# Opening's transposed weights in other tiles, weights' splits behind the scores; no decoding around the middle, lower parts shared out

## The chip, the cores and the metric

The kernel runs on one core of a Trainium2 chip. The metric is the time in device microseconds of that core. Of the kernel before there are three runs: 711.22, 711.5 and 713.99 us, median 711.5 us.

## The reference

Three blocks follow one another; all inputs are float32, apart from the weights of the last block, which the kernel receives in double precision.

```python
# attention: q, k, v of (2, 8, 576, 64)
scores = scale * np.matmul(q, k.transpose(0, 1, 3, 2))
mask_plain = (rel >= 0) & (rel < window)                                       # heads 0-3, window 32
mask_dil = (rel >= 0) & (rel < window * dilation) & (rel % dilation == 0)      # heads 4-7, dilation 4
attn = np.exp(scores - np.max(scores, axis=-1, keepdims=True))                 # masked
attn = attn / (np.sum(attn, axis=-1, keepdims=True) + 1e-09)
x = np.matmul(attn, v)                                                         # -> (1152, 512)
# four experts, all of them computed for every token
for e in range(4):
    h = np.maximum(x @ w1[e], 0.0)            # w1[e] 512 x 1024
    out += p[:, e:e + 1] * (h @ w2[e])        # w2[e] 1024 x 512
# last block
h = x @ w_in                                  # 512 x 2048
g = h - np.tanh(h)
result = g @ w_out                            # 2048 x 512
```

## The kernel before, in words

**Arithmetic.** Each matrix product is three passes of reduced fp32 (type fp32r): an operand is split into a high part (a copy, on ScalarE) and a lower part (a subtraction, on VectorE or GpSimd), and the passes are high x high, high x low, low x high. From the third weight slice on, the first product of a pair is cut in the Strassen-Winograd manner into 7 products of half blocks, whose results are added up on VectorE and GpSimd (`sums_of`; the addition L708 of p5 to u on GpSimd).

**Passes.** The tokens are two sets, g=0 (512 tokens) and g=1 (640). There are 14 passes n, each over one slice of weights: n=0..7 serve set 0 with the experts' 8 slices, n=2..9 set 1 (so n=2..7 serve both, n=8 and 9 only set 1); n=10..13 are the four slices of the last block, called tanh passes here, for both sets. A pass has its h's (14 half products per set, matmuls at L730 for the first two passes and at L782 after) and its y's (one per 128 tokens, 12 matmuls of 128x512 at L825, added to `acc` at L846). `merge` puts the y's of one set between the h's of the other, at the places of `FIRST` and `THEN`.

**Order.** A planner adds up guessed durations of these steps (`duration`, `start`), and everything else is given a due time by `when` and emitted as its due time passes; `later` does the same relative to the step just emitted. Each engine then executes what was emitted in that order. So a table of due times decides what stands before what on VectorE, ScalarE, GpSimd and the SP queue.

**Opening.** `first_attention` runs set 0's four pairs of heads through scores (L480), `largest` (L496), `exps`, `norm` (L519), `transposes` (L527, result copied at L530), `values` (L563) and copying into xf (L567). The result of the transposes lies in the second half t[:, 1] of the same `att` tile that holds the weights; there are four such tiles. Set 1's pairs follow within the first weight passes, one every `BEAT` = 11 planned us.

**Decoding.** w_in and w_out come as doubles. 32 tiles are decoded to fp32: `d_load`, then `d_decode` with one tensor_scalar (L660) and three two-input instructions (L664, L672, L677) on VectorE, one square (L671) on ScalarE, and a store; the list `where` holds the 32 due times.

**Between the experts and the last block.** `x2_step` transposes `acc` into x2f (L871, L875), and `x2_prep` splits it. In the tanh passes `hidden` takes tanh (L762), b - tanh in PSUM (L128), the high part (L769) and the lower part (L128), where `sub` at L128 is the common subtraction.

Of the kernel before, what the change touches and what calls it, by code (L numbers as in the profile page):

```python
# [10 lines left out]
F32R = mybir.dt.float32r  # L11
I32 = mybir.dt.int32
BF16 = mybir.dt.bfloat16
ACTF = mybir.ActivationFunctionType
# [58 lines left out]
def tile_local_attention_moe_tanhshrink(  # L73
# [392 lines left out]
    class Pair:  # L466


        def __init__(self, kind, c, banks):
            self.h, self.c, self.banks = kind, c, banks  # L470
            self.kk = c if kind.plain else 2 + c
            self.n = NST[kind.g]
            self.lag = kind.g
            self.t = {}

# [47 lines left out]
        def transposes(self, a):  # L523
            pb = bank(self.banks["t"])
            t = self.t[a]
            for j in range(4):
                nc.tensor.transpose(  # L527
                    pb[:BK, j * 128:(j + 1) * 128], t[:, 0, j * BK:(j + 1) * BK], ident
                )
            nc.scalar.activation(out=t[:BK, 1], in_=pb[:BK], func=ACTF.Copy)  # L530

# [9 lines left out]
        def values(self, i):  # L541
# [4 lines left out]
            for tile_, j, t, o in h.values()[i]:  # L546
                for a in range(2):
                    f0 = j * 4 * D + (2 * self.c + a) * D
                    n = 32 if tile_ == "short" else BQ
                    if t < 512:  # L550
                        w = self.t[a][:BK, 1, t:t + n]
                    else:
                        w = self.t[0][:BK, 0, a * 128 + t - 512:a * 128 + t - 512 + n]
                    if isinstance(o, tuple):
                        at, step, m = o
                        to = xb[D * a:D * a + D, at:at + step + m]
                        to = xb[D * a:D * a + D, at - 128:at - 128 + 2 * step].rearrange(
                            "c (r p) -> c r p", p=step
                        )[:, :, 128:128 + m]
                        w = w.rearrange("k (r p) -> k r p", p=m)  # L560
                    else:
                        to = xb[D * a:D * a + D, o]
                    nc.tensor.matmul(  # L563
                        out=to, lhsT=h.v[tile_][:BK, f0:f0 + D], rhs=w, start=True, stop=True,
                    )
# [38 lines left out]
    def w_sum(n, name, engine):  # L604
# [9 lines left out]
        else:  # L614
            sub(engine, block(n, "a21"), block(n, "a11"), block(n, "a21"))

    def w1_split(n, name, engine, lag=1.0):
        t = w1t[n, name] = w1p.tile([128, 2, 2, 256], F32R, tag="w1", name="w1")
        src = sums[n] if name in ("s1", "s2", "s4") else block(n, {"s3": "a21"}.get(name, name))
        split(t[:, 0], t[:, 1], src, engine, lag, ("w1", n, name))  # L620
# [121 lines left out]
    def place(g, what):  # L742
# [6 lines left out]
        ring[what] += 1  # L749
        t, i = (store[2], i % 3) if what == "th" else (store[i // 3 % 2], i % 3)  # L750
        return t[:, i * 320:i * 320 + QH[g]]

    def hidden(n, g, f, half, b, done):
# [7 lines left out]
        th = place(g, "th")  # L761
        nc.scalar.activation(out=th, in_=b, func=ACTF.Tanh)  # L762

        def lower():
# [151 lines left out]
    for n in range(N2 + 1, LAST + 1):  # L916
        steps += merge(hs(n, 0), ys(n - 1, 1), FIRST) + merge(hs(n, 1), ys(n, 0), THEN)
    steps += ys(LAST, 1)
# [24 lines left out]
    for n in range(1, len(seq)):  # L943
        after = []
        if n < EARLY:
            t0 = start["h", n - 1, 0, 0]

            for i, name in enumerate(("a11", "a12", "a21", "a22")):
                when(t0 + 5.0 + 1.8 * i, lambda n=n, name=name: w1_split(n, name, nc.gpsimd),
                     ("w1", n, name))  # L950
# [23 lines left out]
    where = []  # L974
    for n, m in [(n, 4) for n in range(EARLY + 1, NS1)] + [(N2, 4), (N2 + 1, 4)]:
        a, b = period(n)
        where += [a + (b - a) * (i + 0.3) / m for i in range(m)]
        if n == NS1 - 1:
            a = start["y", n, 1, 0]
            where += [a + 13.0 * i + 2.0 for i in range(4)]  # L980
    order_d = [o + 4 * s + i for s in range(4) for o in (0, 16) for i in range(4)]
# [10 lines left out]
    for g, due, step in (  # L992
        (0, start["y", NS1 - 1, 1, 0] + 0.1, 5.0),
        (1, start["y", N2 - 1, 1, SETS[1][1] // 128 - 1] + 2.73 + 1.5, 2.8),
# [14 lines left out]
    def first_attention():  # L1009
# [4 lines left out]
        def call(k, stage):  # L1014
            pair, a = head(k)
            getattr(pair, stage)(a)

        pairs[0].scores()
        w1_split(0, "a11", nc.vector)
        pairs[1].scores()  # L1020
        for k in range(8):
            call(k, "largest")
            if k:
                call(k - 1, "norm")
            if k == 1:
                w1_split(0, "a12", nc.gpsimd)
            if k > 1:
# [23 lines left out]
    for n in range(4):  # L1051
        pair = Pair(kinds[1, n < 2], n % 2, {"s": "s", "t": "a", "x": "a"})
        due = BEAT * n
        when(due, pair.scores)
# [11 lines left out]
    for c in range(2):  # L1066
        when(BEAT * 3 + 17.0 + 4.0 * c, lambda c=c: prep(1, c, True, nc.vector, nc.gpsimd), ("x", 1, False))
    for c in range(2):
# [5 lines left out]
    with tc.manual_schedule():  # L1074
# [5 lines left out]
        pa.load_k(0)  # L1080
        w_load(0, 0)
        pa.load_q(slice(1, 2))
        pa.load_k(1)
        w_load(0, 1)
        da.load_q()
        for u in range(2):
            da.load_k_cut(u)
        for i in range(2):
            pa.load_v(i)
        for i in range(2):  # L1090
# [102 lines left out]
```

## Time and profile before

| what | value |
|---|---|
| median of three runs | 711.5 us |
| profiled execution | 711.79 us |
| its span, first to last instruction | 710.0 us |
| TensorE busy | 637.2 us (90%) |
| VectorE busy | 449.0 us (63%) |
| ScalarE busy | 293.7 us (41%) |
| GpSimd busy | 355.9 us (50%) |
| mean granted TensorE clock | 0.945 |

The time outside the span is 1.8 us. The slices of the page show TensorE at 90% or more over most of the span, and lower at the start, near 60% of the span, and at about 70% of it.

### The profile page before, as it was taken

The numbers are of one execution on the slowest core, as the hardware profiler recorded it, in microseconds if no ns is written. First come the engines' busy times: TensorE is split into PE (matmuls) and PEld (weight loads), VectorE is DVE, ScalarE is ACT, GpSimd is POOL, SyncE is SP. The second block draws the span as 40 slices with busy tenths as digits, with TensorE's granted clock in tenths as the row PEclk, the third lists the DMA queues.
The fourth block names the chain that finished last, engine by engine and source line by source line (L and its number), as shares of the span: only waits on it lengthen the run. The fifth ranks groups of instructions, "written<-read, shape, count | busy, mean of one in ns | idle before, by whom it ended". The sixth has DMA issues, their size and how long they took to land.

```text
span 710.0 us, 10901 instructions
## 1 busy us (share of the span) xinstructions
PE 637.2 (90%) x4063; PEld 559.0 (79%) x4063; DVE 449.0 (63%) x892; ACT 293.7 (41%) x656; POOL 355.9 (50%) x319
## 2 busy tenths in 40 slices
PE   5486999899999999999999995969695998999997
PEld 3375787797988989889899893948594887998995
DVE  4449463744795877857858857554757378465672
ACT  2344554534542434424424453332555454353530
POOL 4347596653662733816627478472365354372400
PEclk8658999999999999999999997979898999999999
DMA  8941111201225133242252514231313313200012
GB/s 316 321 133 60 60 61 61 90 0 55 96 69 185 65 128 108 87 161 91 76 177 71 181 46 137 71 104 44 105 45 104 104 45 117 91 31 1 1 45 90
DMA packets 36694, 68.07 MB, mean 96 GB/s; under 512 B 4128, under 2 KB 10400, under 8 KB 36640
## 3 DMA queue, kind: packets, MB, share of 16 engines
q1 hardware_dynamic: 36640, 67.37, 27.9%
q8 instruction: 32, 0.52, 0.3%
q14 instruction: 22, 0.18, 0.1%
HBM read 56.61 MB, written 10.75 MB: 95 GB/s over the span
## 4 chain that ended last, share of the span: by engine, by line
PE 60%; DVE 10%; POOL 6%; issue 3%; ACT 2%; DVEq 0%; POOLq 0%; ACTq 0%
PE bank_f L825 21%; PE bank_f L782 16%; PE bank_s L825 11%; PE bank_s L782 5%; PE bank_a L825 3%; PE bank_a L782 3%; POOL w L128 3%; DVE single L664 1%; POOL sum L128 1%; DVE h L128 1%; DVE single L672 1%; DVE bank_f L708 1%; POOL sums L708 1%; DVE h L714 1%; DVE bank_f L128 1%
## 5 line engine op out<-in xcount | busy, mean ns | idle before, releaser
L825 PE MATMUL bank_f<-w,h 128*128 128x512 f32 x864 | 215.9, 399 | 11.8 <-ACT h L711 7.0
L128 POOL TENSOR_TENSOR w<-raw,w 128x512 fp32r<-128x512 f32 x109 | 145.7, 1340 | 120.6 <-ACT w L165 106.4
L825 PEld LDWEIGHTS bank_f<-w,h 128*128 128x128 f32 x864 | 160.3, 191 | 48.6 <-ACT h L711 8.3
L782 PE MATMUL bank_f<-x,w 128*128 128x320 f32 (+1 forms) x1224 | 182.7, 302 | 2.7 <-DVE h L128 2.2
L782 PEld LDWEIGHTS bank_f<-x,w 128*128 128x128 f32 x1224 | 175.1, 193 | 7.9 <-DVE h L128 2.6
L708 POOL TENSOR_TENSOR sums<-u,p 128x320 f32<-128x320 f32 (+1 forms) x44 | 38.6, 880 | 133.0 <-DVE u L708 133.0
L825 PE MATMUL bank_s<-w,h 128*128 128x512 f32 x324 | 82.9, 406 | 17.2 <-ACT h L769 7.1
L165 ACT ACTIVATE w<-raw 128x512 fp32r<-128x512 f32 x112 | 69.1, 628 | 42.9 <-PE bank_f L825 22.4
L825 PEld LDWEIGHTS bank_s<-w,h 128*128 128x128 f32 x324 | 61.4, 195 | 32.1 <-ACT h L769 7.6
L846 DVE SCALAR_TENSOR_TENSOR acc<-bank_f,pn,acc 128x512 f32<-128x512 f32 x42 | 31.4, 747 | 48.8 <-PE bank_f L825 48.8
L782 PE MATMUL bank_s<-x,w 128*128 128x320 f32 (+1 forms) x396 | 60.2, 297 | 0.6 <-ACT x2f L875 0.6
L782 PEld LDWEIGHTS bank_s<-x,w 128*128 128x128 f32 x396 | 56.4, 189 | 2.5 <-ACT x2f L875 0.9
L128 POOL TENSOR_TENSOR w<-sum,w 128x512 fp32r<-128x512 f32 x36 | 50.3, 1396 | 6.2 <-ACT w L165 6.2
L711 ACT ACTIVATE h<-bank_f 128x320 fp32r<-128x320 f32 (+2 forms) x83 | 35.1, 428 | 43.4 <-DVE bank_f L708 39.1
L714 DVE SCALAR_TENSOR_TENSOR h<-bank_f,h 128x320 fp32r<-128x320 f32 (+2 forms) x83 | 38.9, 473 | 11.4 <-ACT h L711 10.5
L165 ACT ACTIVATE w<-sum 128x512 fp32r<-128x512 f32 x36 | 22.8, 632 | 47.9 <-POOL sum L128 27.8
L794 ACT ACTIVATE p<-bank_f 128x320 f32<-128x320 f32 (+1 forms) x60 | 23.7, 416 | 45.3 <-PE bank_f L782 45.1
L782 PE MATMUL bank_a<-x,w 128*128 128x320 f32 (+1 forms) x228 | 37.2, 299 | 0.1
L782 PEld LDWEIGHTS bank_a<-x,w 128*128 128x128 f32 x228 | 33.7, 191 | 1.6 <-DVE h L714 0.4
L677 DVE SCALAR_TENSOR_TENSOR single<-double,single 128x512 f32<-128x512 f32 x32 | 26.0, 812 | 12.3 <-ACT double L671 11.4
L664 DVE SCALAR_TENSOR_TENSOR single<-double,single 128x512 int32<-128x512 int32 x32 | 32.4, 1013 | 1.1
L730 PE MATMUL bank_f<-x,w 128*128 128x256 f32 x192 | 29.0, 308 | 4.3 <-ACT x L165 4.3
(125 smaller groups left out, 820.7 us busy)
## 6 DMA issues: line engine op xcount, KB each, us to landing
raw<-in_moe_w_dram SPq DMA_DIRECT2D x40, 512.0 KB, 5.3
double<-in_moe_w_in_dram SPq DMA_DIRECT2D x16, 512.0 KB, 3.8
double<-in_moe_w_out_dram SPq DMA_DIRECT2D x16, 512.0 KB, 3.5
in<-single SPq DMA_DIRECT2D x16, 256.0 KB, 2.6
out<-single SPq DMA_DIRECT2D x16, 256.0 KB, 2.1
raw<-in SPq DMA_DIRECT2D x8, 512.0 KB, 6.0
raw<-out SPq DMA_DIRECT2D x8, 512.0 KB, 4.8
h<-in_v_dram SPq DMA_DIRECT2D x7, 512.0 KB, 8.2
```

Source lines behind the costliest of these rows:

```text
L128: engine.tensor_tensor(out=out, in0=a, in1=b, op=ALU.subtract)
L165: nc.scalar.activation(out=hi, in_=src, func=ACTF.Copy)
L664: nc.vector.scalar_tensor_tensor(out=t, in0=high, scalar=-0x40000000, in1=t, op0=ALU.bitwise_and, op1=ALU.bitwise_or)
L677: nc.vector.scalar_tensor_tensor(out=w, in0=mag, scalar=HIGH_MIN * HIGH_MIN, in1=w, op0=ALU.is_ge, op1=ALU.mult)
L708: e.tensor_tensor(out=o, in0=x, in1=y, op=ALU.add)
L711: nc.scalar.activation(out=hi, in_=src, func=ACTF.Relu)
L714: nc.vector.scalar_tensor_tensor(out=lo, in0=src, scalar=0.0, in1=hi.bitcast(F32), op0=ALU.max, op1=ALU.subtract)
L730: nc.tensor.matmul(out=b, lhsT=w[:, wi, kk % 2, f % 2 * 128:(f % 2 + 1) * 128], rhs=x[:, kk % 2, xi, :], start=(kk == 0 and m == 0), stop= ...
L782: nc.tensor.matmul(out=b, lhsT=w[:, wi, kk, t * 128:(t + 1) * 128], rhs=x[:, kk, xi, :], start=(kk == 0 and i == 0), stop=(kk == 1 and i = ...
L794: nc.scalar.activation(out=pt[P], in_=b, func=ACTF.Copy)
L825: nc.tensor.matmul(out=y, lhsT=a, rhs=b_, start=(f == 0 and m == 0), stop=(f == NF - 1 and m == 2),)
L846: nc.vector.scalar_tensor_tensor(out=t, in0=y, scalar=p, in1=t, op0=ALU.mult, op1=ALU.add)
```

## The change

1. The transposed weights of set 0's pairs 0 to 2 go to new tiles "pt" out of the w1 pool, so that an `att` tile is free once it has been transposed and not only after `values`. The tiles of n=0's w1 are placed ahead, and the splits of its first two blocks come behind `largest` of heads 2 and 3; the lower part of both is GpSimd's. The loads stand in another order.
2. The w1 splits of n=1 are due 6 us later, set 1's attention 3 us later.
3. Decoding: 5 tiles a pass instead of 4 in n=3..6, 4 in n=7, none from there to n=11, 5 in n=11 and 3 in n=12 (before: 4 in each of n=3..7, 4 behind n=7, 4 in n=10 and 4 in n=11).
4. Set 0's `x2_step`s are 2.7 planned us apart instead of 5.0.
5. In the tanh passes, for one of the two halves of each block of h, b - tanh is written over the tanh in SBUF, and the lower part is GpSimd's.
6. The first y's of n=11 stand 3 products later.

```diff
@@ transposes
-            nc.scalar.activation(out=t[:BK, 1], in_=pb[:BK], func=ACTF.Copy)
+            if self.lag == 0 and self.kk < 3 and a == 0:
+                far = plain32(w1p.tile([128, 2, 2, 256], F32R, tag="w1", name="pt"))
+                self.pt = {0: far[:, :512], 1: far[:, 512:]}
+            to = self.pt.setdefault(a, t[:, 1])
+            nc.scalar.activation(out=to[:BK], in_=pb[:BK], func=ACTF.Copy)
@@ values
-                        w = self.t[a][:BK, 1, t:t + n]
+                        w = self.pt[a][:BK, t:t + n]
@@ place: where tanh (th) and u5 lie
-        t, i = (store[2], i % 3) if what == "th" else (store[i // 3 % 2], i % 3)
+        t, i = (store[1 + i // 3 % 2], i % 3) if what == "th" else (store[0], i % 3)
@@ hidden
         nc.scalar.activation(out=th, in_=b, func=ACTF.Tanh)
+        if half:
+            def value():
+                sub(nc.vector, th, b, th)
+                done()
+            later(0.8, value, key)
+            later(1.5, lambda: split(hi, lo, th, nc.gpsimd, 0.8, key), key)
+            return
@@ the order of the steps
-        steps += merge(hs(n, 0), ys(n - 1, 1), FIRST) + merge(hs(n, 1), ys(n, 0), THEN)
+        first = FIRST if n > N2 + 1 else (4, 5, 6, 7, 8)
+        steps += merge(hs(n, 0), ys(n - 1, 1), first) + merge(hs(n, 1), ys(n, 0), THEN)
@@ w1 of n=1
-                when(t0 + 5.0 + 1.8 * i, lambda n=n, name=name: w1_split(n, name, nc.gpsimd),
+                when(t0 + 11.0 + 1.8 * i, lambda n=n, name=name: w1_split(n, name, nc.gpsimd),
@@ decoding's due times
-    for n, m in [(n, 4) for n in range(EARLY + 1, NS1)] + [(N2, 4), (N2 + 1, 4)]:
+    for n, m in zip(
+        [*range(EARLY + 1, NS1), N2 + 1, N2 + 2], [5, 5, 5, 5, 4, 5, 3], strict=True
+    ):
...
@@ x2_step
-        (0, start["y", NS1 - 1, 1, 0] + 0.1, 5.0),
+        (0, start["y", NS1 - 1, 1, 0] + 0.1, 2.7),
@@ first_attention
+        for name in ("a11", "a12", "a21", "a22"):
+            w1_place(0, name)
         pairs[0].scores()
-        w1_split(0, "a11", nc.vector)
         pairs[1].scores()
...
-            if k == 1:
-                w1_split(0, "a12", nc.gpsimd)
+            if k in (2, 3):
+                w1_split(0, ("a11", "a12")[k - 2], nc.gpsimd)
@@ set 1's attention
-        due = BEAT * n
+        due = 3.0 + BEAT * n
```

The loads' order shows on the SP queue at the start of the program; x and h are tiles of q, k and v, raw holds expert weights. Before:

```order
L339 DMA x_116<-in_q_dram 128x512
L346 DMA x_118<-in_k_dram 128x544
L598 DMA raw<-in_moe_w_dram 128x2x512
L339 DMA x_116<-in_q_dram 128x512
L346 DMA x_123<-in_k_dram 128x544
L598 DMA raw<-in_moe_w_dram 128x2x512
L339 DMA x_127<-in_q_dram 128x512 x2
L353 DMA x_130<-in_k_dram 128x768
L353 DMA x_132<-in_k_dram 128x768
L360 DMA h_134<-in_v_dram 128x1024
```

And with the change:

```order
L339 DMA x_116<-in_q_dram 128x512
L346 DMA x_118<-in_k_dram 128x544
L339 DMA x_116<-in_q_dram 128x512
L346 DMA x_121<-in_k_dram 128x544
L602 DMA raw<-in_moe_w_dram 128x2x512
L360 DMA h_125<-in_v_dram 128x1024
L360 DMA h_127<-in_v_dram 128x1024
L602 DMA raw<-in_moe_w_dram 128x2x512
L339 DMA x_131<-in_q_dram 128x512 x2
L353 DMA x_134<-in_k_dram 128x768
L353 DMA x_136<-in_k_dram 128x768
```

The second q and k stand ahead of the first weights, and two transfers of v stand ahead of the dilated heads' q and k.

On TensorE, at the end of n=0's h's, the y's of n=0 (L825 before, L844 after) and the transposes of set 1's first pair (L527, into bank_a) change places; L480 are the next pair's scores. Before:

```order
L527 MATMUL bank_a<-ident,att 96x128 x8
L825 MATMUL bank_f<-w_616,h_630 128x512 x3
L825 MATMUL bank_f<-w_636,h_666 128x512 x3
L825 MATMUL bank_f<-w_668,h_717 128x512 x3
L825 MATMUL bank_f<-w_689,h_768 128x512 x3
L480 MATMUL bank_s<-x_151,x_145 64x96 x20
```

And with the change:

```order
L844 MATMUL bank_f<-w_597,h_611 128x512 x3
L844 MATMUL bank_f<-w_613,h_638 128x512 x3
L844 MATMUL bank_f<-w_661,h_711 128x512 x3
L844 MATMUL bank_f<-w_685,h_757 128x512 x3
L527 MATMUL bank_a<-ident,att 96x128 x4
L844 MATMUL bank_f<-w_597,h_611 128x512 x3
```

The first y now stands ahead of both transposes, and the second transpose behind the second y.

On VectorE, in n=8 (names h8_f_1 are this pass's hidden blocks of set 1, L708 adds products, L714 takes the lower part), a decoded tile (single_4517) stood between these before:

```order
L708 TENSOR_TENSOR bank_s_4491<-bank_s_4491,p1_4415 128x320
L660 TENSOR_SCALAR single_4517<-double_4405 128x512
L664 SCALAR_TENSOR_TENSOR single_4517<-double_4405,single_4517 128x512
L714 SCALAR_TENSOR_TENSOR h8_0_1_4488<-bank_s_4479,h8_0_1_4488 128x320
L708 TENSOR_TENSOR bank_a_4508<-bank_a_4508,sums_1420 128x320
L672 SCALAR_TENSOR_TENSOR single_4517<-double_4405,single_4517 128x512
L714 SCALAR_TENSOR_TENSOR h8_1_1_4505<-bank_s_4491,h8_1_1_4505 128x320
L708 TENSOR_TENSOR bank_f_4523<-bank_f_4523,sums_1420 128x320
L714 SCALAR_TENSOR_TENSOR h8_0_1_4488<-bank_a_4508,h8_0_1_4488 128x320
L708 TENSOR_TENSOR u_4459<-bank_f_4538,u_4459 128x320
L708 TENSOR_TENSOR bank_f_4538<-bank_f_4538,sums_1420 128x320
L677 SCALAR_TENSOR_TENSOR single_4517<-double_4405,single_4517 128x512
```

And with the change (L718 and L724 are the former L708 and L714):

```order
L718 TENSOR_TENSOR bank_s_4522<-bank_s_4522,p1_4457 128x320
L724 SCALAR_TENSOR_TENSOR h8_0_1_4519<-bank_s_4511,h8_0_1_4519 128x320
L718 TENSOR_TENSOR bank_a_4536<-bank_a_4536,sums_1402 128x320
L724 SCALAR_TENSOR_TENSOR h8_1_1_4533<-bank_s_4522,h8_1_1_4533 128x320
L718 TENSOR_TENSOR bank_f_4548<-bank_f_4548,sums_1402 128x320
L724 SCALAR_TENSOR_TENSOR h8_0_1_4519<-bank_a_4536,h8_0_1_4519 128x320
L718 TENSOR_TENSOR u_4494<-bank_f_4561,u_4494 128x320
L718 TENSOR_TENSOR bank_f_4561<-bank_f_4561,sums_1402 128x320
```

The four instructions of the decoding are gone from between the hidden blocks.

## Rows read from the trace of the kernel before

**Rows 1.** By windows: us; PE, PEld, DVE, ACT, POOL busy; clock, DMA, GB/s

```profile
0.00:50.70 50.70, 30.59 (x358) 22.31 (x358) 23.78 (x59) 19.12 (x36) 20.22 (x36) 0.68 0.76 259
50.70:85.80 35.10, 27.48 (x223) 23.68 (x220) 24.94 (x46) 15.28 (x32) 23.12 (x25) 0.88 0.22 76
225.50:272.00 46.50, 46.50 (x275) 42.05 (x274) 34.44 (x65) 18.23 (x39) 23.42 (x20) 1.00 0.32 108
413.40:437.10 23.70, 15.26 (x95) 13.77 (x93) 17.20 (x29) 11.82 (x29) 21.59 (x19) 0.87 0.07 23
451.40:473.00 21.60, 14.62 (x98) 13.98 (x96) 13.24 (x23) 9.24 (x21) 18.44 (x15) 0.89 0.08 25
490.00:550.00 60.00, 44.40 (x248) 38.69 (x247) 40.82 (x85) 31.41 (x78) 30.46 (x26) 0.89 0.23 75
550.00:602.00 52.00, 47.81 (x269) 42.52 (x268) 35.27 (x74) 25.17 (x59) 23.18 (x19) 0.97 0.23 80
```

**Rows 2.** The same view while the opening's transfers land

```profile
9.90:16.70 6.80, 3.29 (x68) 2.57 (x68) 6.01 (x14) 2.60 (x5) 4.96 (x6) 0.58 1.04 419
```

**Rows 3.** Timeline, opening: start, us, engine, line, operation, [idle before, releaser]

```profile
9.86 0.89 PE L480 MATMUL bank_f<-x,x 64*64 64x96 f32 x32 [3.95 <-DMA x<-in_k_dram]
...
17.06 1.02 PE L527 MATMUL bank_f<-ident,att 128*96 128x128 f32 x4 [0.22 <-POOL att L519]
...
21.69 0.56 DVE L496 SCALAR_TENSOR_TENSOR att<-bank_s,mask_False 128x384 f32<-128x384 f32 x1 [3.67 <-PE bank_a L563]
...
30.40 0.56 DVE L496 SCALAR_TENSOR_TENSOR att<-bank_f,mask_False 128x384 f32<-128x384 f32 x1 [4.12 <-PE bank_a L563]
...
33.91 1.89 PE L730 MATMUL bank_f<-x,w 128*128 128x256 f32 x6 [3.61 <-ACT x L165]
...
50.68 1.57 PE L730 MATMUL bank_f<-x,w 128*128 128x256 f32 x6
```

**Rows 4.** Timeline of PE in the first pass of tokens with expert weights

```profile
68.67 1.06 PE L527 MATMUL bank_a<-ident,att 128*96 128x128 f32 x4 [2.74 <-ACT att L530]
69.38 4.45 PE L825 MATMUL bank_f<-w,h 128*128 128x512 f32 x12
```

**Rows 5.** The decoding alone, VectorE by windows: us, busy (instructions), clock, DMA

```profile
0.00:710.00 710.00, 107.33 (x128) 0.94 0.28 96
413.40:437.10 23.70, 5.04 (x4) 0.87 0.07 23
451.40:473.00 21.60, 5.34 (x4) 0.89 0.08 25
490.00:504.00 14.00, 2.46 (x4) 0.83 0.00 1
531.00:544.00 13.00, 4.12 (x4) 0.85 0.04 16
```

**Rows 6.** One line of the decoding: ns min/median/max, first and last start

```profile
L664 DVE SCALAR_TENSOR_TENSOR single<-double,single x32: 691/694/1668, 164.5 to 594.3; 128x512 int32<-128x512 int32 x32
```

**Rows 7.** Timeline of PE, pass 8: a stop, and matmuls at the two clocks

```profile
437.14 6.30 PE L825 MATMUL bank_s<-w,h 128*128 128x512 f32 x18 [4.87 <-ACT h L711]
...
443.27 2.88 PE L825 MATMUL bank_a<-w,h 128*128 128x512 f32 x12
```

**Rows 8.** x2's halves (x2f) by windows: VectorE, ScalarE, GpSimd busy, clock, DMA

```profile
413.40:437.10 23.70, 4.89 (x7) 3.17 (x8) 3.76 (x4) 0.87 0.07 23
```

**Rows 9.** Timeline of PE, pass 9

```profile
473.00 2.58 PE L825 MATMUL bank_f<-w,h 128*128 128x512 f32 x5 [6.98 <-ACT h L711]
```

**Rows 10.** Timeline of PE, the first tanh pass

```profile
502.69 1.41 PE L871 MATMUL bank_s<-ident,acc 128*128 128x128 f32 x5 [5.79 <-DVE h L128]
...
543.88 2.93 PE L825 MATMUL bank_s<-w,h 128*128 128x512 f32 x6 [7.13 <-ACT h L769]
```

**Rows 11.** Lines by form, 470 to 710: busy us, mean ns | idle before

```profile
L128 DVE TENSOR_TENSOR h<-bank_f,h 128x320 fp32r<-128x320 f32 x20 | 9.6, 480 | 1.3 <-ACT h L769 1.2
...
L708 POOL TENSOR_TENSOR sums<-u,p 128x320 f32<-128x320 f32 x8 | 7.0, 879 | 6.8 <-DVE u L708 6.8
```

More of the change, by code (lines that the diff above doesn't have):

```diff
@@ L473, in __init__ @@
             self.lag = kind.g
-            self.t = {}
+            self.t, self.pt = {}, {}
         def scores(self):
@@ L615, in w_sum, with w1_place @@
             sub(engine, block(n, "a21"), block(n, "a11"), block(n, "a21"))
+    def w1_place(n, name):
+        t = w1t[n, name] = w1p.tile([128, 2, 2, 256], F32R, tag="w1", name="w1")
+        return t
     def w1_split(n, name, engine, lag=1.0):
-        t = w1t[n, name] = w1p.tile([128, 2, 2, 256], F32R, tag="w1", name="w1")
+        t = w1t.get((n, name))
+        if t is None:
+            t = w1_place(n, name)
         src = sums[n] if name in ("s1", "s2", "s4") else block(n, {"s3": "a21"}.get(name, name))
@@ L974, in tile_local_attention_moe_tanhshrink @@
     where = []
-    for n, m in [(n, 4) for n in range(EARLY + 1, NS1)] + [(N2, 4), (N2 + 1, 4)]:
+    for n, m in zip(
+        [*range(EARLY + 1, NS1), N2 + 1, N2 + 2], [5, 5, 5, 5, 4, 5, 3], strict=True
+    ):
         a, b = period(n)
[L977 to L980, printed above, removed]
+        where += [a + (b - a) * (i + 0.3) / max(m, 5) for i in range(m)]
     order_d = [o + 4 * s + i for s in range(4) for o in (0, 16) for i in range(4)]
@@ L1066, in tile_local_attention_moe_tanhshrink @@
     for c in range(2):
-        when(BEAT * 3 + 17.0 + 4.0 * c, lambda c=c: prep(1, c, True, nc.vector, nc.gpsimd), ("x", 1, False))
+        when(BEAT * 3 + 20.0 + 4.0 * c, lambda c=c: prep(1, c, True, nc.vector, nc.gpsimd), ("x", 1, False))
     for c in range(2):
@@ L1080, in tile_local_attention_moe_tanhshrink @@
         pa.load_k(0)
-        w_load(0, 0)
         pa.load_q(slice(1, 2))
         pa.load_k(1)
+        w_load(0, 0)
+        for i in range(2):
+            pa.load_v(i)
         w_load(0, 1)
@@ L1087, in tile_local_attention_moe_tanhshrink @@
             da.load_k_cut(u)
-        for i in range(2):
-            pa.load_v(i)
         for i in range(2):
```

## The prediction, made before the changed kernel ran

> **What bounds the kernel now.** I read four views in this order: the busy slices of the page, the windows by stage, the timeline at each place where the slices fall, and last the lines by form for prices. The windows are to be read for TensorE's busy time against the length [rows 1]. In the expert period 225.5 to 272 us it is busy 46.50 of 46.50: there the matmuls are the time, VectorE has 34.44 busy and 12 us to spare, and nothing that the change does to other engines can save anything. The idle time lies in six other windows: 20.1 of 50.7 us in the opening, 7.6 of 35.1 in the first expert pass, 8.4 of 23.7 in pass 8, 7.0 of 21.6 in pass 9, 15.6 of 60 in the last block's beginning (x2, first tanh pass) and 4.2 of 52 in the second. The sum is 62.9 us, and this is all that the change can work on. The granted clock is 0.68, 0.88, 0.87, 0.89, 0.89 and 0.97 there, against 1.00 in the expert period, so a filled gap gives back something of the clock as well.
>
> In the opening the transfers are the first limit: between 9.9 and 16.7 us they move 419 GB/s at a DMA share of 1.04 [rows 2]. The second is a ring of tiles: the timeline [rows 3] has VectorE's L496 of head 4 at 21.69 after 3.67 us of waiting for `values` (L563), and of another head at 30.40 after 4.12 us for the same. The first product L730 that needs x comes at 33.91, the whole of n=0's h's goes on from 50.68. In pass 1 TensorE waits 2.74 us at 68.67 for a copy of transposes, and the first y stands behind that in the queue [rows 4].
>
> **Opening.** The two waits of 3.67 and 4.12 us are for an `att` tile that `values` still reads; with the transposed weights in tiles of their own it is free after the transposes, and 7.8 us of waiting go. What is late next is the data. Loads: x of pair 1's k was in SBUF at 9.86; ahead of it on the queue stood 0.52 MB of weights, which now come after, so it lands 0.52 MB / 419 GB/s = 1.3 us sooner, which helps VectorE's first steps alone. The dilated q and k were complete 1.83 MB after that k (0.52 of weights, 0.52 of q, 0.79 of k, by the tiles' sizes on the queue), so at 9.86 + 1.83/0.419 = 14.2 us; the two v transfers (1.05 MB, 2.5 us) now stand ahead of them, so 16.7. On TensorE the transposes of head 1 stand behind the scores of that dilated pair; they began at 17.06 and now can at 16.7 + 0.6 of scores = 17.3. So 0.2 us of the 7.8 is lost there, and I give back 1.6 more because with the ring gone ScalarE, VectorE and GpSimd, which have 19.1 to 23.8 us of work each in 50.7 [rows 1], work through the same heads closer together. The splits of w1's a11 and a12 wait behind heads 2 and 3 in the order; the products that use them come at 33.9, so they are hidden. Taken: -6.0. Bounds: -7.8, if nothing is late next, and +2.5, if the whole chain hangs on the dilated loads.
>
> **First pass.** The first y of n=0 no longer stands behind the transposes that waited 2.74 us, and set 1's attention is 3 us later in the plan, behind n=0's h's. The window has 7.6 us idle, of which GpSimd (23.1 busy of 35.1 [rows 1]) keeps a part for n=1's splits. Taken -2.0, bounds -5.0 and 0.
>
> **Pass 8.** Decoding costs VectorE 107.33 us for 128 instructions, so 3.35 us a tile [rows 5]. The tile in this window cost 5.04, since GpSimd works nearly without a pause there (21.59 of 23.70 [rows 1]); the line L664 has a median of 694 ns and a maximum of 1668 [rows 6]. TensorE's stop before 437.14 is 4.87 us, waiting for a hidden block, and after it 18 matmuls take 6.30 us (350 ns each) where 12 soon afterwards take 2.88 (240 ns each): 18 x 110 = 2.0 us are the clock's [rows 7]. With the decoding gone from between the hidden blocks VectorE loses 5.0 us of this chain; GpSimd loses the four halves of x2 that stood between the weights' splits, 3.76 us [rows 8], because x2 is now done within the y's before. The two chains lie beside each other, so I count the shorter with 0.7 more for the stretched instructions of GpSimd that get their normal time, 4.5 in all, and 1.5 of the 2.0 of the clock. Taken -6.0, bounds -8.4 (the whole idle time) and -2.
>
> The Trainium skill (SBUF — State Buffer, "SBUF: two separate sides") says that a VectorE instruction with two inputs in SBUF and a GpSimd instruction that reads SBUF hold a common port in turn, each for its whole length. The trace's 691 ns beside 1668 for one and the same instruction agrees with that. By the rule the lower parts that go to GpSimd would also lengthen each decoding beside them by up to about 1 us, an estimate from the two ends of that row; it changes no term below by more than its bounds.
>
> **Pass 9.** Its tile cost 5.34 [rows 5] where 2.46 is the price alone; TensorE stops 6.98 us before 473.00 [rows 9]. VectorE has idle time there (13.24 busy of 21.60), GpSimd less (18.44), so only what stood in the last part of the chain counts, about half of the tile's time: -3.0; bounds -5.3 and -1.0.
>
> **x2 and the first tanh pass.** Two stops: 5.79 us before 502.69 and 7.13 before 543.88 [rows 10]. Before the first the decoding takes 2.46 (window 490 to 504), before the second 4.12 (531 to 544) [rows 5]. In that second window VectorE has no pause and goes from hidden block to hidden block, so its 4.12 are in the chain; of the 2.46 I count half, 1.2. The four lower parts per set that leave VectorE cost 0.48 us each [rows 11] (set 1; set 0's no more), 1.9 us for set 1. Against that GpSimd gets them at 0.88 (its price for another two-input addition of 128x320 [rows 11]), 3.5 us a set, with 30.46 busy of 60 [rows 1]; and the hidden block that waits for it comes 0.4 later. 4.1 + 1.2 + 1.9 = 7.2; I take off 2.2 for GpSimd, which becomes the later one for the last hidden blocks of set 1. Taken -5.0, bounds -11 (15.6 idle less what x2's own transposes need) and +2.
>
> **Second tanh pass and later.** n=11 has 5 tiles instead of 4: +3.35 on VectorE; eight lower parts leave it: -3.8 at 0.48. GpSimd has 23.18 busy of 52, so 8 x 0.88 = 7.0 fits. The first y's three products later give the last hidden blocks of n=10's set 1 that much more time. Taken 0, bounds -4 (the idle time, 4.2) and +3. Three tiles in n=12 and four more over n=3..6 stand beside matmuls: VectorE rises there from 34.4 to 34.4 + 3.35 = 37.8 of 46.5, which is still cover. Were it gone, each would cost its 3.35 whole. I take +1.5 for all seven, and +0.5 for x2's steps, whose transposes follow each other at 2.7 and whose bank must be copied out by ScalarE first; bounds 0 and +10 for both.
>
> **Sum.** -6.0 - 2.0 - 6.0 - 3.0 - 5.0 + 0 + 2.0 = -20.0, against the profiled execution 711.8 (span 710.0 and 1.8 around it): 691.8. That execution lies 0.3 above the median of the runs, so 691.5.
>
> **Rivals.**
> 1. The opening gives nothing. For it: the DMA share of 1.04, and 2.5 us of v ahead of the dilated q and k. Against it: the two waits are for tiles, at 21.7 and 30.4, long after the loads. Without its 6.0: 697.5, and with +2.5: 700.
> 2. GpSimd becomes the bound in the tanh passes. All 32 lower parts cost it 32 x 0.88 = 28 us where VectorE had 15.4; if those of one pass (7.0) come on the path in n=11 and the gain of n=10 is lost: 691.5 + 5.0 + 7.0 = 703.5. For it: GpSimd has the splits of the next weights in the same queue. Against it: it is idle half the time in these windows. A rule of the Trainium skill (GPSIMD Engine Reference, "4.1 Engine selection") gives elementwise work to VectorE, as GpSimd takes some twice as long for two inputs; the trace's 879 against 480 ns agrees.
> 3. Slower than before: VectorE, with a fifth tile of decoding in the expert periods and three in n=12, falls behind TensorE until no PSUM bank is free. Eight tiles are moved into stretches where TensorE has no idle time. If each costs its 3.35 us there, 26.8, the kernel ends at 711.5 - 20.0 + 26.8 = 718.3. It decides from 2.5 us of path per moved tile (20.0 / 8). Against it: 8.7 us of pause per period remain. For it: the pauses are an average, and a tile's two-input instructions come in one piece of up to 5.3 us.
> 4. Rivals 1 and 2 together: 691.5 + 6.0 + 12.0 = 709.5, no change.
>
> **Chances.** Forecast 0.64 (its own range 684 to 698: six terms, whose bounds lie 2 to 8 us away and are not met together, so about 7 us each way), rival 1 0.12, rival 2 0.12, rivals 1 and 2 together 0.05, rival 3 0.07. A difference within 0.5%, 3.6 us here, can't be told from no change. So faster 0.88, no change 0.05 (the fourth), slower 0.07 (the third). The range goes from 681 (the forecast's own end less 3, half of the room that the tanh pass's bound of -11 leaves) to 704, which takes in the first two rivals.
>
> **What would show it.** Opening right: L496 of heads 4 and 6 with no wait for L563, the first L730 with x near 27, n=0's h's going on near 44 to 45. First pass: the first y ahead of the transposes, without a stop of 2.7. Pass 8: no `single` row in the window, TensorE's stop before the first y under 2 us, the matmuls after it near 240 ns. Tanh pass: the stop of 7.13 down to some 3 us; GpSimd's lower parts near 0.88. The expert periods still at 46.5 us with TensorE at 100%. The forecast is wrong if these periods grow, if GpSimd is the releaser of the first y's in n=11 and after, or if the h's of n=0 go on later than 48.

## The result, and the profile after

The changed kernel takes 701.47 us (median of 4 runs, 700.26 to 703.06) against 712.06 us of the kernel before (711.22 to 713.99): a ratio of 0.985, with an interval of 0.982 to 0.988. So it is faster by 10.6 us. The direction was forecast and the time lies in the range; the gain is half of the 20 us forecast. The profiled execution took 700.26 us with a span of 698.4, 11.6 less than before, and the granted clock is 0.953 on average where it was 0.945.

To see where the time went, I follow four instructions that both programs have, in the timeline of each: the first instruction of the first decoded tile in pass 3 (VectorE), the first transposes of x2 of set 0, the first product of pass 10 that waits for x2 (TensorE), and the last y of set 0 in pass 11. Before:

```profile
163.63 0.83 DVE L660 TENSOR_SCALAR single<-double 128x512 int32<-128x512 int32 x1
...
396.68 0.49 PE L871 MATMUL bank_s<-ident,acc 128*128 128x128 f32 x3
...
494.49 1.69 PE L782 MATMUL bank_s<-x,w 128*128 128x256 f32 x12 [0.64 <-ACT x2f L875]
...
599.81 1.03 PE L825 MATMUL bank_f<-w,h 128*128 128x512 f32 x3 [1.54 <-ACT h L769]
```

And after (first the first product with x, which answers to 33.91 in [rows 3]):

```profile
26.00 1.90 PE L740 MATMUL bank_f<-x,w 128*128 128x256 f32 x6 [1.00 <-ACT x L165]
...
155.99 0.83 DVE L670 TENSOR_SCALAR single<-double 128x512 int32<-128x512 int32 x1
...
398.08 0.49 PE L890 MATMUL bank_s<-ident,acc 128*128 128x128 f32 x3
...
488.40 1.69 PE L801 MATMUL bank_s<-x,w 128*128 128x256 f32 x12 [0.64 <-ACT x2f L894]
...
585.32 1.65 PE L844 MATMUL bank_f<-w,h 128*128 128x512 f32 x3 [3.76 <-ACT h L788]
```

The differences at these points and at the end of the span give what each stretch gained (minus) or lost, here for the change and for those kernels of the next section that tell a stretch apart, each against the kernel before:

| stretch | change | e1 | e2 | e3 | e4 | e7 | e8 | f2 |
|---|---|---|---|---|---|---|---|---|
| opening to pass 3 | -7.6 | -7.4 | -0.7 | -8.5 | -8.4 | -8.0 | -7.5 | -9.5 |
| passes 3 to 7 | +9.0 | -0.7 | +7.8 | -0.1 | +9.0 | +7.5 | +9.0 | -0.7 |
| passes 8 and 9 | -7.5 | -7.8 | -4.2 | +0.4 | -7.8 | -4.3 | -7.4 | -5.9 |
| x2, passes 10 and 11 | -8.4 | -10.5 | -4.9 | +0.2 | -11.5 | -7.1 | -2.3 | -12.7 |
| passes 12 and 13 | +2.9 | +3.9 | +3.5 | 0.0 | +4.8 | +3.9 | +3.1 | +3.8 |
| whole span | -11.6 | -22.5 | +1.5 | -7.9 | -13.9 | -7.9 | -5.1 | -25.1 |

Each column is one profiled execution, and the times of one kernel differ: by 2.8 us between the four runs of the change, by 4.5 in e7 and by 7.4 in e8. So differences of 1 to 2 us between columns say little. The loss in the expert passes is the main thing; it is there, at 7.5 to 9.0 us, in every kernel with the table's fifth tiles where they were. The list of TensorE's waits between 160 and 390 us (us in total, times, longest) had one line before, of 0.4 us; now it has four stops for hidden blocks, one in each of passes 3 to 6. Before, and after:

```profile
PE bank_f L825 <- DVE h L714: 0.4, 2, 0.2
```

```profile
PE bank_f L844 <- ACT h L721: 3.4, 2, 1.7
PE bank_a L844 <- ACT h L721: 1.8, 1, 1.8
PE bank_s L844 <- ACT h L721: 1.7, 1, 1.7
```

The timeline at the first of them, VectorE, ScalarE and TensorE:

```profile
200.91 1.08 DVE L670 TENSOR_SCALAR single<-double 128x512 int32<-128x512 int32 x1
202.03 1.66 DVE L674 SCALAR_TENSOR_TENSOR single<-double,single 128x512 int32<-128x512 int32 x1
203.61 0.49 DVE L718 TENSOR_TENSOR bank_s<-bank_s,u 128x320 f32<-128x320 f32 x1
...
204.34 0.42 ACT L721 ACTIVATE h<-bank_s 128x320 fp32r<-128x320 f32 x1
...
204.81 1.02 PE L844 MATMUL bank_a<-w,h 128*128 128x512 f32 x3 [1.81 <-ACT h L721]
...
206.69 4.16 PE L844 MATMUL bank_f<-w,h 128*128 128x512 f32 x12
```

Two instructions of a decoded tile, 2.74 us together, stand in VectorE's queue ahead of the addition that completes the pass's last hidden block; ScalarE's copy follows it and TensorE's y waits 1.81 us. In this case the next 12 matmuls take 4.16 us, and the window over them (columns as in [rows 1]) has a granted clock of 0.67, that is between the two levels of 1.2 and 2.4 GHz:

```profile
206.70:210.80 4.10, 4.10 (x14) 3.28 (x14) 0.00 (x0) 0.38 (x1) 0.00 (x0) 0.67 0.96 309
```

The tile is the fifth of the five of its pass. After the other three stops 12 matmuls take 2.91 us. The stops make 6.9 of the 9.0. Where no such slow matmuls follow any of them (e7, granted clock 1.00 in all of passes 3 to 7), the loss is 7.5; so some 1.5 of the 9.0 are the clock's.

The other stops. In pass 8 the decoding is gone from the window, but a stop of 5.39 us before the first y remains (4.87 in [rows 7]): ScalarE's queue now waits 5.01 us for a sum of weights from GpSimd, with the copies of hidden blocks behind it. In the first tanh pass the stops of 5.79 and 7.13 [rows 10] are 2.48 and 1.35; between them two stops of 0.53 and 0.33 have become 1.57 and 1.34. A new stop of 3.76 stands in pass 11 (585.32, above).

```profile
428.79 0.63 ACT L165 ACTIVATE w<-sum 128x512 fp32r<-128x512 f32 x1 [5.01 <-POOL sum L128]
...
433.93 6.38 PE L844 MATMUL bank_s<-w,h 128*128 128x512 f32 x18 [5.39 <-ACT h L721]
...
493.29 1.33 PE L890 MATMUL bank_s<-ident,acc 128*128 128x128 f32 x5 [2.48 <-DVE sums L128]
...
534.64 1.90 PE L844 MATMUL bank_f<-w,h 128*128 128x512 f32 x6 [1.35 <-ACT h L788]
```

### The profile page after: what moved, and what is told of

It is laid out like the page before. It is cut to its first block, busy times and chain, and to the rows that moved or that the text cites. A ratio compares the mean times of both kernels' runs of the same rounds, so it can differ in the third digit from the quotient of the medians.

```text
span 698.4 us, 10894 instructions
## 1 busy us (share of the span) xinstructions
PE 638.0 (91%) x4063; PEld 558.7 (80%) x4063; DVE 449.2 (64%) x859; ACT 289.7 (41%) x656; POOL 387.3 (55%) x352
## 5 line engine op out<-in xcount | busy, mean ns | idle before, releaser
L844 PE MATMUL bank_f<-w,h 128*128 128x512 f32 x864 | 225.3, 409 | 25.5 <-ACT h L721 10.3
L844 PEld LDWEIGHTS bank_f<-w,h 128*128 128x128 f32 x864 | 164.1, 197 | 66.4 <-ACT h L721 12.6
L128 POOL TENSOR_TENSOR w<-raw,w 128x512 fp32r<-128x512 f32 x110 | 149.5, 1365 | 87.2 <-ACT w L165 79.5
L718 POOL TENSOR_TENSOR sums<-u,p 128x320 f32<-128x320 f32 (+1 forms) x44 | 40.3, 919 | 126.5 <-DVE u L718 124.6
L844 PE MATMUL bank_s<-w,h 128*128 128x512 f32 x312 | 77.8, 400 | 7.9 <-ACT h L721 7.1
L844 PEld LDWEIGHTS bank_s<-w,h 128*128 128x128 f32 x312 | 58.6, 193 | 21.1 <-ACT h L721 7.9
L724 DVE SCALAR_TENSOR_TENSOR h<-bank_f,h 128x320 fp32r<-128x320 f32 (+2 forms) x83 | 38.8, 473 | 14.4 <-ACT h L721 13.9
L681 ACT ACTIVATE double<-double 128x512 f32<-128x512 f32 x32 | 21.8, 681 | 43.8 <-DVE single L674 35.6
L674 DVE SCALAR_TENSOR_TENSOR single<-double,single 128x512 int32<-128x512 int32 x32 | 38.8, 1211 | 1.1
L718 DVE TENSOR_TENSOR u<-bank_f,p 128x320 f32<-128x320 f32 (+1 forms) x31 | 14.1, 456 | 26.5 <-PE bank_f L801 20.1
```

The lines of the kernel that those rows point to most:

```text
L128: engine.tensor_tensor(out=out, in0=a, in1=b, op=ALU.subtract)
L674: nc.vector.scalar_tensor_tensor(out=t, in0=high, scalar=-0x40000000, in1=t, op0=ALU.bitwise_and, op1=ALU.bitwise_or)
L681: nc.scalar.activation(out=mag, in_=mag, func=ACTF.Square)
L718: e.tensor_tensor(out=o, in0=x, in1=y, op=ALU.add)
L724: nc.vector.scalar_tensor_tensor(out=lo, in0=src, scalar=0.0, in1=hi.bitcast(F32), op0=ALU.max, op1=ALU.subtract)
L844: nc.tensor.matmul(out=y, lhsT=a, rhs=b_, start=(f == 0 and m == 0), stop=(f == NF - 1 and m == 2),)
```

## The experiments

Each was timed in three rounds beside the kernel before; ratios are to that kernel, with their interval.

**e1: the fifth tile of passes 3 to 6 behind the last hidden block.** From the changed kernel:

```diff
+        late = 0.4 if n < NS1 else 0.0
-        where += [a + (b - a) * (i + 0.3) / max(m, 5) for i in range(m)]
+        where += [a + (b - a) * (i + 0.3 + late * (i == 4)) / max(m, 5) for i in range(m)]
```

> The changed kernel, with the fifth decoded tile of passes 3 to 6 due 3.7 planned us later, behind the last hidden block of set 1 instead of ahead of it; as many tiles as before in each pass. Theory (place): the four stops of 1.7 to 1.8 us of TensorE at 204.8, 255.5, 304.5 and 353.6 us go, the expert passes lose at most 1 us against the kernel before instead of 9, and the time is 694 us (691 to 697). Rival (count): five tiles are too many for VectorE in these passes, so the stops come back at other hidden blocks and the time stays at 700 to 702 us.

Measured: 689.5 us, 0.968 [0.965, 0.970]. TensorE's list of waits between 160 and 385 us is empty, the stretch loses nothing (-0.7), with the same number of tiles. The timeline at the place of the first stop:

```profile
201.14 0.49 DVE L718 TENSOR_TENSOR bank_s<-bank_s,u 128x320 f32<-128x320 f32 x1
201.66 0.44 ACT L721 ACTIVATE h<-bank_s 128x320 fp32r<-128x320 f32 x1 [0.53 <-DVE bank_s L718]
...
202.54 0.93 DVE L670 TENSOR_SCALAR single<-double 128x512 int32<-128x512 int32 x1
...
204.48 2.91 PE L844 MATMUL bank_f<-w,h 128*128 128x512 f32 x12
```

The tile comes after the addition, and the 12 matmuls take 2.91 us. So the place costs the 9 us, not the count. The time is below my 691 to 697: I had counted the four stops (7 us), and the stretch gains 9.7 on the changed kernel, its slow matmuls included, and x2 with passes 10 and 11 another 2.1. These 2.1 are mostly the clock's: the stops there are the same within 0.2 us each, and the granted clock is 0.97 (478.5 to 573.4) instead of 0.94; why is not shown.

**e2: the table of decoding alone.** The kernel before with the changed `where`.

```diff
-    for n, m in [(n, 4) for n in range(EARLY + 1, NS1)] + [(N2, 4), (N2 + 1, 4)]:
+    for n, m in zip([*range(EARLY + 1, NS1), N2 + 1, N2 + 2], [5, 5, 5, 5, 4, 5, 3], strict=True):
```

> The kernel before with the new table of decoding times alone. Theory: the table has both the gain of passes 8 to 10 (about -5, -2 and -5 us) and the loss of passes 3 to 6 (+9) and of passes 11 and 12 (+3 to +6): together about 711 to 713 us, no change. Rival: the loss in the expert passes has to do with the other edits (their earlier start); then the table alone gains: 699 to 703 us.

Measured: 714.8 us, 1.004 [1.002, 1.005], slower by 0.4% where I had expected 711 to 713 and no change. The table alone gains 9.1 us around the middle and loses 11.3 on both sides of it. The loss belongs to the table.

**e3: the opening alone.** The kernel before with the new tiles, the loads' order, the new places of n=0's splits, and the shifts of n=1's splits and set 1's attention.

```diff
+            to = self.pt.setdefault(a, t[:, 1])
...
-        due = BEAT * n
+        due = 3.0 + BEAT * n
```

> The kernel before with the opening alone: the new tiles, the order of the loads, the splits of the first two passes' w1 and set 1's attention 3 us later. Theory: 13 us ahead at the end of the first pass, 5 to 6 of them given back before pass 2 because GpSimd's splits and the attention of set 1 are not sooner, so 704 us (702 to 706). Rival: what is given back comes from the other edits and the 13 us stay: 698 to 699 us.

Measured: 702.5 us, 0.986 [0.984, 0.989]. 8.5 us, all of it before pass 3, and none given back after that. Before pass 3 it went as I expected: the first y of n=1 starts 13.9 us sooner (90.99 instead of 104.91; a part of set 1's attention now stands behind it), pass 2's first product only 6.0 sooner (113.35 instead of 119.39).

**e4 and f3: all lower parts on VectorE.** e4 is the changed kernel with `hidden` and `place` as before, f3 is e1 with `hidden` as before.

```diff
-        if half:
-            def value():
-                sub(nc.vector, th, b, th)
-                done()
...
```

> The changed kernel with all lower parts of the tanh passes on VectorE as before, and tanh's tiles as before. Theory: the lower parts on GpSimd are a gain of 3 to 6 us in passes 10 to 13, and without them the time is 704 to 707 us. Rival: the first tanh pass gained by the decoding alone and GpSimd's lower parts, at 0.88 us instead of 0.48, cost as much as they give: 700 to 702 us, or less.

> The kernel with the fifth tiles later (e1_fifth_later), with all lower parts of the tanh passes on VectorE as before (tanh's places as in the changed kernel). Theory (GpSimd's lower parts give nothing): 687 to 690.5 us, no difference to 689.5 beyond 0.3%. Rival (they are the gain of the tanh passes): 692 to 696 us.

Measured: e4 697.9 us, 0.981 [0.977, 0.984], f3 688.9, 0.967 [0.965, 0.968] beside e1's 0.968. My theory for e4 fell. The lower parts on GpSimd bring nothing: from x2 to the end e1 gains 6.6 us and f3 6.0, e4 6.7 and the change 5.5. On VectorE (e4) the first tanh pass has stops of 4.13, 0.53 and 0.33 us where the change has 2.48, 1.57 and 1.34: what the first gains, the next two lose. Of e4's 3.6 us in the medians 0.8 stands in the opening of the profiles, where it has no other instruction than the changed kernel.

**f1 and f2: pass 11's fifth tile moved as well.** f1 is e1 with the tiles 5, 5, 5, 5, 5, 4, 3; f2 is that with f3's lower parts.

```diff
-        [*range(EARLY + 1, NS1), N2 + 1, N2 + 2], [5, 5, 5, 5, 4, 5, 3], strict=True
+        [*range(EARLY + 1, NS1), N2 + 1, N2 + 2], [5, 5, 5, 5, 5, 4, 3], strict=True
```

> The kernel with the fifth tiles later (e1_fifth_later), and the fifth tile of pass 11 moved to pass 7, likewise behind the last hidden block: tiles 5, 5, 5, 5, 5, 4, 3. Theory (place): the stop of 3.75 us at 573.4 us in that kernel, whose VectorE queue shows the same picture as the expert passes, goes, and so do the slow matmuls behind it: 685 us (684 to 687). Rival: a tile at the end of pass 7 holds up x2 or the hidden blocks of pass 8, which costs 3 to 5 us again: 688 to 690 us.

> Both: pass 11's fifth tile in pass 7, and all lower parts on VectorE. Theory: the two don't touch each other, so 683 to 687 us, the fastest. Rival: with its eight lower parts a pass back, VectorE has no room for even four tiles in pass 11 and three in pass 12, and stops stay: 688 to 691 us.

Measured: f1 687.2 us, 0.963 [0.961, 0.966]; f2 686.8, 0.964 [0.962, 0.965]. In f1 the stop of 3.75 is 1.44, near the 1.54 of the kernel before, so the tile made it. Whether by its place or by the count this doesn't tell, since pass 11 has one tile fewer. Passes 8 and 9 gain 6.0 instead of e1's 7.8, but f3, which has no tile there, gains 6.4; so that the tile beside x2 takes anything back is not shown. f1's time lies just above the range of its theory, f2's in the range of its own. The stop in f1:

```profile
574.04 1.02 PE L844 MATMUL bank_f<-w,h 128*128 128x512 f32 x3 [1.44 <-ACT h L788]
```

**e5 and g1: set 1's attention 3 us earlier,** in the changed kernel (e5) and in f2 (g1).

```diff
-        due = 3.0 + BEAT * n
+        due = BEAT * n
...
```

> The changed kernel with set 1's attention due as before (0 + 11 n instead of 3 + 11 n). Theory: the 13 us that are gained by 91 us and the 5 to 8 that are given back between 91 and 110 us both come of the attention standing later behind the first hidden blocks; earlier, it is a gain of 8 to 10 at 91 us and nothing is given back: the same 701 to 702 us at the end. Rival (the later attention is a loss): 697 to 699 us. Rival (it is the gain): 704 to 706 us.

> The fastest so far (f2_both) with set 1's attention due as before, 3 us earlier. Theory: the two stops of 0.7 and 3.2 us at 93 to 98 us go, at the price of the stops of 2.5 and 2.0 us at 55 to 58, and 3 to 5 us stay: 682 us (681 to 684). Rival: the gain seen with the earlier attention alone was a matter of how small VectorE instructions happened to fall beside GpSimd's: 686 to 687 us.

Measured: e5 696.5 us, 0.977 [0.976, 0.979]; g1 686.5, 0.962 [0.961, 0.964], no more than f2. My theory for e5 (no difference) fell, and so did its first rival when g1 showed no gain on f2: what came about is g1's rival, 686 to 687. Of e5's 5 us on the changed kernel, 2.7 lie before pass 3 and 1.5 in passes 3 to 7, where it has the same four stops (1.67 to 1.87 us) but no matmuls at a lower clock. In g1 pass 2's first product starts 2.3 us sooner than in f2 (110.02 and 112.31), pass 3's first decoded tile no sooner (154.25 and 154.12). Under the last heading is a VectorE instruction of set 1's attention that takes 2.33 us in some kernels and 1.08 in others; that it decides between e5 and the change is not shown.

**e6: the loads as before,** in the changed kernel.

```diff
+        w_load(0, 0)
         pa.load_q(slice(1, 2))
         pa.load_k(1)
-        w_load(0, 0)
...
```

> The changed kernel with the opening's loads in the former order. Theory (the v transfers ahead of the dilated q and k cost 2.5 us at the first dilated scores, which is made up by the chain behind): 700 to 703 us, the first product with x at 25 to 27 us. Rival (the new order is the larger part of the opening's gain): first product with x at 30 or later, 705 us or more.

Measured: 697.9 us, 0.979 [0.976, 0.981], less than I expected. The first product with x starts at 24.54, 1.5 us before the changed kernel's; L496 of head 4 starts at 14.73 instead of 17.06, near the 2.5 us that I had put on the v transfers. The rival falls: the new order is no part of the gain. What is, the next section says.

**e7: x2 as before.**

```diff
-        (0, start["y", NS1 - 1, 1, 0] + 0.1, 2.7),
+        (0, start["y", NS1 - 1, 1, 0] + 0.1, 5.0),
```

> The changed kernel with set 0's x2 steps 5.0 planned us apart as before, so that x2's halves stand between pass 8's weight splits on GpSimd again, with no decoding there. Theory (GpSimd's queue sets the end of pass 8, since its stop of 5.4 us is still there without the decoding): 3 to 4 us of the gain of passes 8 and 9 go: 704 to 706 us. Rival (the decoding on VectorE was the whole gain): 701 to 702 us.

Measured: 701.5 us, 0.982 [0.979, 0.985], the median of the changed kernel. But in the profile the stretch of passes 8 and 9 gains 4.3 instead of 7.5, and its stop is 7.05 us, with the decoding gone in both:

```profile
434.93 5.24 PE L844 MATMUL bank_s<-w,h 128*128 128x512 f32 x12 [7.05 <-ACT h L721]
```

The share of x2's steps is thus 3.2 of the 7.5 in these two executions. That it comes by way of GpSimd is argued from the order of the queues; x2's halves cost all three engines 3.2 to 4.9 us there [rows 8]. The medians don't show the share: e7's four runs lie at 699.4, 699.8, 703.1 and 703.9 (the profiled one), and what sets the two pairs apart I can't attribute.

**e8: pass 11's first y's as before.**

```diff
-        first = FIRST if n > N2 + 1 else (4, 5, 6, 7, 8)
+        first = FIRST if n > N2 + 1 else FIRST
```

> The changed kernel with pass 11's first y's after 1 to 5 products as in the other passes. Theory (they wait for the hidden blocks of pass 10, set 1): a stop of 2 to 4 us at 535 us, 703 to 706 us. Rival (these blocks are ready in time without the decoding): no difference, 700 to 702 us.

Measured: 705.3 us (699.26 to 706.69), 0.987 [0.982, 0.992]. One of the four runs is shorter than the changed kernel's, so the time alone doesn't decide. In the profile (706.7, one of the longest) the stop before pass 11's first y is 3.48 instead of 1.35, later one of 1.31 comes, and x2 and passes 10 and 11 gain 2.3 instead of 8.4.

```profile
534.78 2.93 PE L844 MATMUL bank_s<-w,h 128*128 128x512 f32 x6 [3.48 <-ACT h L788]
...
560.72 4.66 PE L801 MATMUL bank_f<-x,w 128*128 128x320 f32 x30 [1.31 <-DVE sums L128]
```

## Why the prediction was right in direction and half wrong in size

**The step that failed** is the cost of the tiles that are added elsewhere: "Three tiles in n=12 and four more over n=3..6 stand beside matmuls: VectorE rises there from 34.4 to 34.4 + 3.35 = 37.8 of 46.5, which is still cover." I took +1.5 for all seven. Measured: +9.0 in passes 3 to 7 and +2.9 in passes 12 and 13. Of the 2.9, 1.7 are new stops in pass 12 (the longer one below); the rest are matmuls behind pass 11's stop of 3.76, at a granted clock of 0.73 (585.3 to 590.9), and belong to pass 11's fifth tile, whose term was 0. So the seven tiles cost 10.7 in place of 1.5. The forecast's own sign of being wrong, that the expert periods grow, came about. The cover is an average over the period; what counts is the place in VectorE's queue. Four fifth tiles at 0.86 of the period stood ahead of the last hidden block, and each stopped TensorE for 1.7 to 1.8 us. With the same tiles a little later (e1) the loss is gone, so the busy time was right and the inference from it wrong. Rival 3 had the engine and the sign, and its "for it" named the cause: the pauses are an average, and a tile's instructions come in one piece. Its condition, that no PSUM bank is free, did not hold in passes 3 to 6, where TensorE waits for a copied hidden block; in pass 12 it did, for 1.5 us. There a product into bank_s waits until VectorE has read that bank, with the four instructions of a tile standing among the additions ahead (602.53 to 607.39). No run moved that tile:

```profile
608.97 0.41 DVE L128 TENSOR_TENSOR h<-bank_s,h 128x256 fp32r<-128x256 f32 x1
...
609.43 1.14 PE L801 MATMUL bank_s<-x,w 128*128 128x320 f32 x6 [1.53 <-DVE h L128]
```

**Opening and first pass:** -8.0 forecast, -7.6 measured (-8.5 alone). L496 of heads 4 and 6 start at 17.06 and 22.17 (21.69 and 30.40 in [rows 3]), neither with a wait for L563, and x's first product at 26.00 where I had said near 27. But the tiles are not the whole of it. Before, the split of w1's a11 stood ahead of L496 of head 0 in VectorE's queue, which was idle for 5.49 us until that split could start:

```profile
9.03 0.69 DVE L128 TENSOR_TENSOR w<-raw,w 128x512 fp32r<-128x512 f32 x1 [5.49 <-ACT w L165]
9.64 0.55 DVE L496 SCALAR_TENSOR_TENSOR att<-bank_s,mask_True 128x384 f32<-128x384 f32 x1
```

Now it starts at 6.15 (first line below), and at 6.27 in e6, whose loads stand as before. So 3.5 of the 7.9 us by which x's first product is sooner come from the split's new place, for which the forecast had nothing, and the other 4.4 come where the two waits were, for which it had 7.8 less 1.8. No run has the tiles without the split's new place. That the sum fits is in part luck. Later too it went otherwise than I described. n=0's h's end 9.3 us sooner (51.62 instead of 60.88), pass 2's first product starts only 5.2 sooner (114.19 instead of 119.39): three new stops for hidden blocks (54.50 and two more, of 1.16 and 1.68 us) take the place of the one for transposes [rows 4], and two follow before pass 2:

```profile
6.15 0.56 DVE L496 SCALAR_TENSOR_TENSOR att<-bank_s,mask_True 128x384 f32<-128x384 f32 x1 [2.60 <-PE bank_s L480]
...
17.06 0.56 DVE L496 SCALAR_TENSOR_TENSOR att<-bank_s,mask_False 128x384 f32<-128x384 f32 x1 [2.71 <-PE bank_s L480]
...
22.17 0.54 DVE L496 SCALAR_TENSOR_TENSOR att<-bank_f,mask_False 128x384 f32<-128x384 f32 x1
...
54.50 1.23 PE L844 MATMUL bank_f<-w,h 128*128 128x512 f32 x3 [1.49 <-ACT h L721]
...
93.37 0.97 PE L844 MATMUL bank_f<-w,h 128*128 128x512 f32 x3 [0.74 <-DVE h L724]
...
97.56 0.79 PE L844 MATMUL bank_f<-w,h 128*128 128x512 f32 x1 [3.22 <-DVE h L724]
```

**Passes 8 and 9:** -9.0 forecast, -7.5 measured. Subtracted at the ends of the two stops (437.14 and 473.00 before, 433.93 and 467.19 after), pass 8 has -4.6 for -6.0 and pass 9 -2.6 for -3.0. With the decoding gone and x2 as before (e2 and e7), pass 8 gains 1.7 and pass 9 2.4; x2's steps give pass 8 another 2.9. So in pass 8 I had the chain wrong: the decoding was not what TensorE's stop of 4.87 hung on. It held up an earlier stop of 3.49 us, which the forecast doesn't name and which is gone now. The stop of 4.87 hung on ScalarE, whose queue waited for a sum of GpSimd's, and it did not shrink to 2 us but is 5.39. Before:

```profile
429.79 2.48 PE L825 MATMUL bank_s<-w,h 128*128 128x512 f32 x6 [3.49 <-DVE h L714]
...
435.78 0.63 ACT L165 ACTIVATE w<-sum 128x512 fp32r<-128x512 f32 x1 [1.96 <-POOL sum L128]
```

I was wrong, too, that the shorter of the two chains alone counts: with the decoding gone, x2's steps still gave their share. The steps alone, with the decoding left in, were not run.

**x2 and passes 10 and 11:** -5.0 and 0 forecast, -8.4 measured. I had given the later first y's nothing; by the one profile of e8 they are some 6 of it, 3.4 in stops and most of the rest in matmuls at a granted clock of 0.87 (533 to 560 us) instead of 1.00. The times alone don't separate e8 from the change. The lower parts on GpSimd are worth nothing, near the 1.9 gained less 2.2 lost that I had put; rival 2 did not come about, GpSimd at 0.88 to 0.90 us for 128x320 kept up (lines by form, after, 470 to 710 us, columns as in [rows 11]):

```profile
L128 POOL TENSOR_TENSOR h<-x,h 128x320 fp32r<-128x320 f32 x8 | 7.1, 898 | 6.3 <-ACT h L165 6.3
...
L128 POOL TENSOR_TENSOR h<-sums,h 128x320 fp32r<-128x320 f32 x8 | 7.0, 877 | 4.7 <-ACT h L165 4.7
```

In sum, the opening, passes 8 and 9, and x2 with passes 10 and 11 gained 23.5 us where their terms came to -22.0; the other stretches lost 11.9 where I had +2.0 (with 0.5 for x2's steps). The time lies in the forecast range because that was wide enough to take in two rivals, not because the sum was right.

Better than both kernels are f2 and g1, at 686.8 and 686.5 us, 0.964 and 0.962 of the kernel before.

## What to carry to other kernels

An engine's pause per period doesn't say what an added instruction costs; look in its queue for what stands behind the instruction and how soon another engine needs that. Put filler work behind the last result that the bottleneck waits for, not at even distances. A change made of a gain and a loss shows its parts when the times at a few fixed instructions of both traces are subtracted.

## What the runs showed of the hardware

A VectorE addition of 128x4 or 128x5 takes 166 ns in the median and 2328 at most in the changed kernel. The row of that line (ns min/median/max), and the timeline of the longest, beside two GpSimd instructions that follow each other:

```profile
L516 DVE TENSOR_TENSOR sm<-sm,eps x16: 161/166/2328, 9.4 to 113.2; 128x4 f32<-128x4 f32 x8, 128x5 f32<-128x5 f32 x8
```

```profile
89.94 1.30 POOL L128 TENSOR_TENSOR w<-sum,w 128x512 fp32r<-128x512 f32 x1
90.18 2.33 DVE L516 TENSOR_TENSOR sm<-sm,eps 128x5 f32<-128x5 f32 x1
...
91.20 1.29 POOL L128 TENSOR_TENSOR w<-raw,w 128x512 fp32r<-128x512 f32 x1
92.54 0.19 DVE L517 RECIPROCAL sm<-sm 128x5 f32<-128x5 f32 x1
92.65 0.67 DVE L724 SCALAR_TENSOR_TENSOR h<-bank_f,h 128x512 fp32r<-128x512 f32 x1
```

It begins after the first and ends at 92.51, with the second's end at 92.49. In f3 the same addition has the same two neighbours and takes 1.08:

```profile
90.01 1.29 POOL L128 TENSOR_TENSOR w<-sum,w 128x512 fp32r<-128x512 f32 x1
90.24 1.08 DVE L516 TENSOR_TENSOR sm<-sm,eps 128x5 f32<-128x5 f32 x1
...
91.26 1.30 POOL L128 TENSOR_TENSOR w<-raw,w 128x512 fp32r<-128x512 f32 x1
91.36 0.19 DVE L517 RECIPROCAL sm<-sm 128x5 f32<-128x5 f32 x1
```

There it ends as the first neighbour does. The hidden block's lower part (L724) behind it starts 1.19 us sooner (91.46). That a tiny instruction with two inputs waits for whole GpSimd instructions agrees with the Trainium skill (SBUF — State Buffer, "SBUF: two separate sides"), which has such instructions hold a common port in turn for their whole length. What decides between one neighbour and two was not tested. Kernels that differ only later in the program fell on either side: f1, f2 and f3, with 1.08, were timed on one chip, and e1, e3, e4, e6, e7 and e8, with 2.33 to 2.34, on two others, so the chip can't be told from chance. Nor does this instruction alone set the opening's time: f1 and e4 both gain 8.4 us before pass 3, with 1.08 and 2.33.
